# Bias off TensorE, transposes spread between matmuls, and a reordered first block in a gated SSM + MLP kernel

## Chip, cores, metric

One core of one Trainium2 chip. The metric is device microseconds of one execution. The span of a profiled run is some 1.7 us shorter than its time.

The profiles name the engines: PE is TensorE (PEld its weight loads), DVE VectorE, ACT ScalarE, POOL GpSimd, SP SyncE. PE writes into eight PSUM banks, `ps`; an eviction is the copy from a bank to SBUF. The granted clock is the share of full TensorE clock that the profile records. Names in the lines: `xnat` x as loaded, `xn` its layernorm, `xt` and `xnt` their transposes; `btres` B transposed; `u` the evicted B projection; `gt` the gelu output; `ht` the scanned state; `tq` the gated MLP output; `r` beside `in_A_C_re` or `in_A_C_im` a C load, one part of C; `wst` a staging buffer that holds a transposed part of C until it is stored to `ct_scratch`. A line that reads `[0.67 <-ACT xnt L428]` says that the engine was idle for 0.67 us before it, until that instruction. Some matmul records are missing from the traces, so x15 can stand for 16, with a gap of about 0.2 us in place of the missing one. The parts and items 1 to 7 are those of the prediction.

## The reference

```python
# x: 1 x 2048 x 1024 bf16; B_w1: 1024 x 3584; B_w2: 3584 x 1024
g = sigmoid((x * gate_w).sum(-1, keepdims=True))
# A: a diagonal complex recurrence between two complex projections
Bu   = einsum("bld,pd->blp", x, B_bar)
h[t] = Lam_bar * h[t-1] + Bu[:, t]                  # 2048 steps, 1024 channels
a    = 2 * einsum("blp,dp->bld", hseq, C).real + x * Dskip
# B: layernorm and an MLP
b    = gelu(layernorm(x) @ B_w1 + B_b1) @ B_w2 + B_b2
out  = g * a + (1 - g) * b
```

## The kernel before

The sequence is cut into four blocks of 512 rows. Each block runs `bu` (the B projection, 8 x 16 matmuls), `m1` (28 tiles, gelu on ScalarE), then for each half of the output columns `m2` (the second MLP matmul) and `my` (the C projection). VectorE runs the scan (`chain`). The first block also builds tables (Sin on ScalarE, products `CG` on VectorE) and transposes B (`bprep`) and C (`cprep`). Everything is ordered by hand: in the traces an instruction that waits also holds up those emitted after it on its engine (m_wst1 and i1_cload below show it for ACT and for the Pool queue).

```python
def load_x(self, b):                       # one transfer of 1 MB
    self.dma(q, ..., self.Xnat[:, :, :], src, writes=["xnat"])

def tx(self, b, part, banks=(6, 7)):       # 4 x 8 transposes, evicted by ACT
    for s in range(4):
        bank = banks[s % 2]
        ...

def cprep(self, i, banks):                 # one staging buffer
    ...
    Wst = self.Wst
    def t0(): ...ACT: Wst[:, 0, :] <- ps...
    def t1(): ...ACT: Wst[:, 1, :] <- ps..., then Pool queue: CTd <- Wst
    self.pending_act.extend([t0, t1])      # one is taken after each m1 tile

def m2(self, b, dblk, hook=None):
    def body0(h):                          # bias: ones (1 x 128) times b2row (1 x 512)
        for s in range(4):
            ins = h.matmul(self.ps[:, s, :], self.onesb[0:1, 0:128], self.b2row[...], start=True, stop=False)
    self.op(pe, body0, ..., writes=[f"ps{s}" for s in range(4)])
    for c in range(14):                    # 8 matmuls each
        ...
        if hook is not None and c == hook[0]: hook[1]()
    for s in range(4):                     # eviction by ACT
        self.op(act, lambda h: h.activation(self.TQ[s], self.ps[:, s, :], ACTF.Identity, scale=omg), ...)

# build(), cuts
cprep_at = {2: 0, 5: 1, 9: 2, 12: 3, 16: 4, 19: 5, 23: 6, 26: 7}   # m1 tile: C transpose
for b in range(NB):
    for i in range(8):
        ev = self.bu(b, i, defer_evac=(i >= 6))
        ...
    if b == 0: self.tx(0, 1, banks=(4, 5))
    for f in range(NF):
        self.m1(b, f)
        if deferred and f in (0, 4):
            i, ev = deferred.pop(0); ev()
            if b == 0 and i == 7: self.table_act(7); self.table_cg(7)
            self.chain(b, i)
        if b == 0 and f in cprep_at: ...   # after every second one: the next C load, Pool queue
    ...
    self.m2(b, 0); self.my(b, 0)
    self.m2(b, 1, hook=(6, all four transposes of xn))
    self.my(b, 1, hook=(0, all four transposes of x))
```

The table scratch lies in tiles 16 to 27 of the gelu output `gt`; the scratch of the products is gt tile 19, so the gelu of tile 19 must wait for the last `table_cg`.

Of the kernel before, what the change touches and what calls it, by code (L numbers as in the profile page):

```python
# [7 lines left out]
F32 = mybir.dt.float32  # L8
BF16 = mybir.dt.bfloat16
# [56 lines left out]
class _Builder:  # L66
# [96 lines left out]
    def alloc(self):  # L163
# [5 lines left out]
        self.rows = sb("rows", [64, 128], BF16)  # L169
        self.b2row = sb("b2row", [1, 1024], BF16)  # L170
        self.gwbc = sb("gwbc", [128, 1024], BF16)
# [44 lines left out]
        self.CTd = nc.dram_tensor("ct_scratch", [16, 128, 1024], BF16)  # L216

        self.psTb = [self.ps[:, k, :].bitcast(BF16) for k in range(8)]
        self.psT = [self.psTb[6], self.psTb[7]]
# [50 lines left out]
    def setup_rows_dma(self):  # L270
        rows = self.rows
        vecs = [(self.Lre_in, 0, 8), (self.Lim_in, 8, 8), (self.ldt_in, 16, 8), (self.Dsk_in, 24, 8), (self.b1_in, 32, self.NF)]
        items = [(rows[r0:r0 + n, :], ap.rearrange("(i p) -> i p", p=128), ["rows"]) for ap, r0, n in vecs]
        self.dma_group(self.sp, "d_rows", items)
        items = [(self.gwbc[:, :], self.gw_in.rearrange("(o n) -> o n", o=1).partition_broadcast(128), ["gwbc"]),
                 (self.b2row[:, :], self.b2_in.rearrange("(o n) -> o n", o=1), ["b2row"])]
        self.dma_group(self.act, "d_cst", items)
        self.mark_const("gwbc", "b2row")

# [94 lines left out]
    def load_x(self, b):  # L374
        src = self.x2[b * 512:(b + 1) * 512, :].rearrange("(s p) d -> p s d", p=128)
        q = self.sp if b == 0 else self.pool
        self.dma(q, "d_x" if b == 0 else "d_xp", self.Xnat[:, :, :], src, writes=["xnat"])

    def ln_stats(self, b):
        dve, pool = self.dve, self.pool  # L380
        Xn, XN = self.Xnat, self.XN
        for s in range(4):
            for hh in range(2):
                self.op(dve, lambda h, s=s, hh=hh: h.bn_stats(self.lnst[:, s, hh * 6:(hh + 1) * 6], Xn[:, s, hh * 512:(hh + 1) * 512]),  # L384
                        reads=["xnat"], writes=[f"lnst{s}"])
            self.op(dve, lambda h, s=s: h.bn_aggr(self.lnmv[:, s, :], self.lnst[:, s, :]), reads=[f"lnst{s}"], writes=[f"lnmv{s}"])
# [4 lines left out]
        for s in range(4):  # L391
            self.op(dve, lambda h, s=s: h.tensor_scalar(XN[:, s, :], Xn[:, s, :], self.lnmv[:, s, 0:1], self.rstd[:, s:s + 1],
                                                      ALU.subtract, ALU.mult),
                    reads=["xnat", f"lnmv{s}", "rstd"], writes=[f"xn{s}"])

    def gate_z(self, b):
        dve = self.dve
        Xn = self.Xnat
        for s in range(4):
            self.op(dve, lambda h, s=s: h.scalar_tensor_tensor(self.junk, Xn[:, s, :], 1.0, self.gwbc[:, :], ALU.mult, ALU.mult,  # L400
                                                             accum_out=self.zc[:, b % 2, s:s + 1]),
                    reads=["xnat", "gwbc"], writes=["q1", f"zc{b % 2}_{s}"])

# [8 lines left out]

    def tx(self, b, part, banks=(6, 7)):
        pe, act = self.pe, self.act
        src = self.Xnat if part == 0 else self.XN
        srcnames = ["xnat"] if part == 0 else [f"xn{s}" for s in range(4)]
        dst = self.XT if part == 0 else self.XNT
        dstname = "xt" if part == 0 else "xnt"
        for s in range(4):
            bank = banks[s % 2]  # L420

            def body(h, s=s, bank=bank):
                ins = None
                for k in range(8):
                    ins = h.transpose(self.psTb[bank][:, k * 128:(k + 1) * 128], src[:, s, k * 128:(k + 1) * 128], self.ident[:, :])  # L425
                return ins
            self.op(pe, body, reads=srcnames + ["ident"], writes=[f"ps{bank}"])
            self.op(act, lambda h, s=s, bank=bank: h.activation(dst[:, :, s * 128:(s + 1) * 128],  # L428
                                                               self.psTb[bank].rearrange("p (k n) -> p k n", k=8), ACTF.Identity),
                    reads=[f"ps{bank}"], writes=[dstname])  # L430

# [25 lines left out]
    def cprep(self, i, banks):  # L457
# [10 lines left out]
        nre, nim = f"ps{banks[0]}", f"ps{banks[1]}"  # L468
        Wst = self.Wst

        def t0():
            self.op(act, lambda h: h.activation(Wst[:, 0, :], pre, ACTF.Identity, scale=2.0), reads=[nre], writes=["wst_re"])

        def t1():
            self.op(act, lambda h: h.activation(Wst[:, 1, :], pim, ACTF.Identity, scale=-2.0), reads=[nim], writes=["wst_im"])
            dst = self.CTd.ap().rearrange("(c i) p d -> i p c d", c=2)[i]
            self.dma(pool, "d_ctw", dst, Wst[:, :, :], reads=["wst_re", "wst_im"], writes=[f"ctd{i}", f"ctd{8 + i}"])
        self.pending_act.extend([t0, t1])
# [121 lines left out]

    def m2(self, b, dblk, hook=None):
        pe, act = self.pe, self.act
        NC2 = self.NF // 2

        def body0(h):
            ins = None
            for s in range(4):
                ins = h.matmul(self.ps[:, s, :], self.onesb[0:1, 0:128], self.b2row[0:1, dblk * 512:(dblk + 1) * 512], start=True, stop=False)  # L608
            return ins
        self.op(pe, body0, reads=["onesb", "b2row"], writes=[f"ps{s}" for s in range(4)])  # L610
        for c in range(NC2):
            view, names = self.w2_load(dblk, c)
            last = (c == NC2 - 1)

            def body(h, c=c, view=view, last=last):
                ins = None
                for s in range(4):
                    for ff in range(2):
                        ins = h.matmul(self.ps[:, s, :], self.GT[:, 2 * c + ff, s * 128:(s + 1) * 128], view[:, ff, :],  # L619
                                       start=False, stop=(last and ff == 1))  # L620
                return ins
            self.op(pe, body, reads=names + [f"gt{2 * c}", f"gt{2 * c + 1}"], writes=[f"ps{s}" for s in range(4)])
            if hook is not None and c == hook[0]:
                hook[1]()
        for s in range(4):
            omg = self.omgcol[:, 4 * b + s:4 * b + s + 1]
            self.op(act, lambda h, s=s, omg=omg: h.activation(self.TQ[s], self.ps[:, s, :], ACTF.Identity, scale=omg),  # L627
                    reads=[f"ps{s}", f"omg{b}"], writes=[f"tq{s}"])

    def my(self, b, dblk, hook=None):  # L630
        pe, dve, act = self.pe, self.dve, self.act
        xt = self.XT

        def body0(h):
# [8 lines left out]
        for c in range(8):  # L643
# [10 lines left out]
            self.op(pe, body, reads=names + [f"ht{2 * c}", f"ht{2 * c + 1}"], writes=[f"ps{4 + s}" for s in range(4)])  # L654
            if hook is not None and c == hook[0]:
                hook[1]()
        for s in range(4):
# [7 lines left out]
    def build(self):  # L665
# [14 lines left out]
        self.bprep_load(6)  # L680
        self.bprep_load(7)
        self.setup_b()
        for i in range(8):
            self.table_dve(i)
        for c in range(3):
            self.w1_chunks[(0, c)] = self.w1_load(c)
        cprep_at = {2: 0, 5: 1, 9: 2, 12: 3, 16: 4, 19: 5, 23: 6, 26: 7}
        for b in range(NB):
            deferred = []
            for i in range(8):  # L690
# [3 lines left out]
                if b == 0:  # L694
                    if i + 2 < 8:
                        self.bprep(i + 2)
                    if i >= 1:
                        self.table_act(i - 1)
                        self.table_cg(i - 1)
                        if i - 1 <= 5:  # L700
                            self.chain(0, i - 1)
                    if i == 3:
                        self.setup_diag()
# [4 lines left out]
            if b == 0:  # L708
                self.tx(0, 1, banks=(4, 5))
            for f in range(NF):  # L710
                self.m1(b, f)
                if deferred and f in (0, 4):
                    i, ev = deferred.pop(0)
                    ev()
                    if b == 0 and i == 7:
                        self.table_act(7)
                        self.table_cg(7)
                    self.chain(b, i)
                if b == 0 and f in cprep_at:
                    ci = cprep_at[f]  # L720
                    self.cprep(ci, (6, 7) if ci % 2 == 0 else (0, 1))
                    if ci % 2 == 1 and ci + 1 < 8:
                        self.cprep_load((ci + 1) // 2)
            self.drain_act(len(self.pending_act))
# [10 lines left out]
            self.my(b, 0)  # L735
            hook_m2 = (6, (lambda b=b: self.tx(b + 1, 1, banks=(4, 5)))) if b + 1 < NB else None
            self.m2(b, 1, hook=hook_m2)

            def hook_fn(b=b):
                self.tx(b + 1, 0, banks=(0, 1))  # L740
            hook_my = (0, hook_fn) if b + 1 < NB else None
            self.my(b, 1, hook=hook_my)
            if b + 2 < NB:
                self.load_x(b + 2)
        fin = [_Tok(self.dma_sems[n], self.dma_counts[n], "dma") for n in self.dma_sems]
# [67 lines left out]
```

## Time and profile before

| | before |
|---|---|
| time, 6 runs | 706.22 us median (705.39 to 709.84) |
| span of the profiled run | 706.9 us |
| PE / DVE / ACT busy | 94% / 50% / 29% |
| first B projection, first m1, first m2 start (PE timeline) | 18.88, 58.68, 127.48 us |

The three starts divide the first block, where most of PE's listed waits lie (23.7 of 30.9 us). The prediction below shows the lines.

### The profile page before, as it was taken

Reading aid. Unit: us, or ns where it says so; the run is one execution under the profiler, and the core shown is the slowest. Engines: PE = TensorE matmul, PEld = TensorE weight load, DVE = VectorE, ACT = ScalarE, POOL = GpSimd, SP = SyncE. Lnnn points to the kernel's source line nnn. Section 1 sums busy time; section 2 is a strip of 40 time slices with the busy share of each in tenths; the row PEclk is TensorE's granted clock in tenths of the full one; section 3 lists DMA queues with packets and bytes.
Section 4 is the critical chain, followed back from the end, with each engine's and each line's share of the span. In section 5 each row is a group of like instructions: output and inputs, shape, how many; then the busy total and the mean of one; then the engine's idle time right before and its main releaser. Section 6 shows DMA issues by size and latency. Waiting matters only on the chain.

```text
span 706.9 us, 8889 instructions
## 1 busy us (share of the span) xinstructions
PE 667.2 (94%) x3489; PEld 317.0 (45%) x3489; DVE 351.0 (50%) x840; ACT 207.9 (29%) x281; POOL 38.2 (5%) x63
## 2 busy tenths in 40 slices
PE   3998898899999999999999999999999999999994
PEld 2554444344444444444444444444444444444442
DVE  4799998331005999811004999830102999300101
ACT  4886745110231243201231243301131233401010
POOL 1010121001001000000001000000101000000101
PEclk9999999899999999999999999999999999999998
DMA  8611676545435055444436045444534035444520
GB/s 282 210 61 45 226 252 228 203 149 167 131 97 172 1 147 151 149 150 154 142 96 203 0 117 151 150 151 148 164 105 149 0 89 151 149 153 146 175 64 30
DMA packets 113894, 97.33 MB, mean 138 GB/s; under 512 B 4923, under 2 KB 107323, under 8 KB 113852
## 3 DMA queue, kind: packets, MB, share of 16 engines
q1 hardware_dynamic: 109050, 80.77, 37.4%
q0 software_dynamic: 4656, 15.73, 6.0%
q8 instruction: 27, 0.44, 0.2%
q10 hardware_dynamic: 146, 0.26, 0.2%
q14 instruction: 15, 0.12, 0.1%
HBM read 88.36 MB, written 8.39 MB: 137 GB/s over the span
## 4 chain that ended last, share of the span: by engine, by line
PE 80%; DVE 13%; ACT 3%; DMA 2%; issue 1%; POOL 0%; DVEq 0%; ACTq 0%; POOLq 0%
PE ps L619 28%; PE ps L592 22%; PE ps L651 16%; PE ps L494 12%; DVE g L543 3%; PE ps L608 1%; DMA xnat<-in_A_x_dram 1%; PE ps L639 1%; PE ps L425 1%; ACT xt L428 1%; ACT xnt L428 1%; DVE lnst L384 1%; DVE p L518 1%; DVE q L549 1%; DVE p L519 1%
## 5 line engine op out<-in xcount | busy, mean ns | idle before, releaser
L592 PE MATMUL ps<-xnt,ring 128*128 128x512 bf16 x896 | 199.1, 384 | 7.1 <-ACT gt L597 5.4
L619 PE MATMUL ps<-ring,gt 128*128 128x512 bf16 x896 | 197.6, 382 | 0.0
L660 DVE SCALAR_TENSOR_TENSOR r<-ps,gcol,r 128x512 bf16<-128x512 f32 x32 | 21.8, 744 | 300.4 <-PE ps L651 300.4
L592 PEld LDWEIGHTS ps<-xnt,ring 128*128 128x128 bf16 x896 | 88.0, 99 | 113.8 <-issue 6.4
L619 PEld LDWEIGHTS ps<-ring,gt 128*128 128x128 bf16 x896 | 87.4, 98 | 108.7 <-issue 6.8
L597 ACT ACTIVATE gt<-ps,cst 128x512 bf16<-128x512 f32 x112 | 76.8, 687 | 128.4 <-PE ps L592 122.5
L494 PE MATMUL ps<-xt,btres 128*128 128x512 bf16 x512 | 113.5, 382 | 0.3 <-ACT btres L449 0.3
L651 PE MATMUL ps<-ring,ht 128*128 128x512 bf16 x512 | 112.3, 379 | 0.0
L494 PEld LDWEIGHTS ps<-xt,btres 128*128 128x128 bf16 x512 | 50.1, 99 | 60.2 <-issue 1.6
L651 PEld LDWEIGHTS ps<-ring,ht 128*128 128x128 bf16 x512 | 49.7, 98 | 57.8
L627 ACT ACTIVATE r<-ps,omgcol 128x512 f32<-128x512 f32 x32 | 19.4, 688 | 131.8 <-PE ps L619 131.8
L501 ACT ACTIVATE u<-ps 128x1024 bf16<-128x1024 f32 x32 | 32.7, 1023 | 83.3 <-PE ps L494 81.6
L543 DVE TENSOR_TENSOR_SCAN g<-dc,zmid,wb 128x256 bf16<-128x256 f32 x64 | 44.6, 738 | 1.1
L428 ACT ACTIVATE xnt<-ps 128x1024 bf16<-128x1024 bf16 x16 | 16.4, 1024 | 79.7 <-PE ps L425 78.6
L147 POOL DMA_DIRECT2D out_dram<-r x32 | 17.5, 547 | 392.5 <-DVE r L660 390.0
L543 DVE TENSOR_TENSOR_SCAN g<-dc,z,wb 128x256 bf16<-128x256 f32 x48 | 33.3, 734 | 0.0
L384 DVE BATCH_NORM_STATS2 lnst<-xnat 128x6 f32<-128x512 bf16 x32 | 21.5, 673 | 16.1 <-DMA xnat<-in_A_x_dram 15.5
L518 DVE TENSOR_TENSOR p<-u,CGre 128x1024 bf16<-128x1024 bf16 x32 | 22.0, 687 | 5.7 <-ACT u L501 5.3
L548 DVE TENSOR_TENSOR q<-g,Ere 128x1024 bf16<-128x1024 bf16 x32 | 22.1, 691 | 1.1
L425 PE MATMUL ps<-ident,xnat 128*128 128x128 bf16 x128 | 10.8, 242 | 12.2 <-DMA xnat<-in_A_x_dram 8.4
L519 DVE TENSOR_TENSOR p<-u,CGim 128x1024 bf16<-128x1024 bf16 x32 | 21.9, 684 | 0.0
L549 DVE TENSOR_TENSOR q<-g,Eim 128x1024 bf16<-128x1024 bf16 x32 | 21.9, 683 | 0.0
(104 smaller groups left out, 345.5 us busy)
## 6 DMA issues: line engine op xcount, KB each, us to landing
ring<-in_B_w_dram SPq DMA_DIRECT2D x56, 512.0 KB, 3.7
ring<-in_B_w_dram SPq DMA_DIRECT2D x112, 256.0 KB, 2.8
ring<-ct_scratch SPq DMA_DIRECT2D x64, 256.0 KB, 2.6
ct_scratch<-wst POOLq DMA_DIRECT2D x8, 512.0 KB, 4.0
out_dram<-r POOLq DMA_DIRECT2D x32, 128.0 KB, 2.3
xnat<-in_A_x_dram POOLq DMA_DIRECT2D x3, 1024.0 KB, 5.8
r<-in_A_C_re_dram POOLq DMA_DIRECT2D x4, 512.0 KB, 5.5
r<-in_A_C_im_dram POOLq DMA_DIRECT2D x4, 512.0 KB, 7.0
```

The costliest lines, as they stand in the source:

```text
L384: self.op(dve, lambda h, s=s, hh=hh: h.bn_stats(self.lnst[:, s, hh * 6:(hh + 1) * 6], Xn[:, s, hh * 512:(hh + 1) * 512]), reads=["xnat"], ...
L428: self.op(act, lambda h, s=s, bank=bank: h.activation(dst[:, :, s * 128:(s + 1) * 128], self.psTb[bank].rearrange("p (k n) -> p k n", k=8) ...
L494: ins = h.matmul(self.ps[:, 2 * pair + c, :], self.BTres[:, i, k, c * 128:(c + 1) * 128], xt[:, k, :], start=(k == 0), stop=(k == 7))
L501: self.op(act, lambda h: h.activation(self.U[u][:, :, :], self.ps[:, 2 * pair:2 * pair + 2, :], ACTF.Identity), reads=[f"ps{2 * pair}", f" ...
L518: self.op(dve, lambda h: h.tensor_tensor(v4(P1), v4(U), CGre_b, ALU.mult), reads=[f"u{u}", f"CG{i}"], writes=["p1"])
L519: self.op(dve, lambda h: h.tensor_tensor(v4(P2), v4(U), CGim_b, ALU.mult), reads=[f"u{u}", f"CG{i}"], writes=["p2"])
L543: self.op(dve, lambda h, c=c, init=init, hf=hf: h.tensor_tensor_scan(G[:, c, hf * TT:(hf + 1) * TT], rb, Wb[:, c, hf * TT:(hf + 1) * TT], ...
L549: self.op(dve, lambda h: h.tensor_tensor(v4(Q2), v4(G), Eim_b, ALU.mult), reads=[f"g{gs}_0", f"g{gs}_1", f"Ei{i}"], writes=["q2"])
L592: ins = h.matmul(self.ps[:, bank, :], view[:, k, ff * 128:(ff + 1) * 128], self.XNT[:, k, :], start=(k == 0), stop=(k == 7))
L597: self.op(act, lambda h: h.activation(self.GT[:, f, :], self.ps[:, bank, :], ACTF.Gelu_apprx_tanh, bias=b1c), reads=[f"ps{bank}", "cst"], ...
L619: ins = h.matmul(self.ps[:, s, :], self.GT[:, 2 * c + ff, s * 128:(s + 1) * 128], view[:, ff, :], start=False, stop=(last and ff == 1))
L651: ins = h.matmul(self.ps[:, 4 + s, :], self.HT[:, 2 * c + pp, s * 128:(s + 1) * 128], view[:, pp, :], start=False, stop=(last and pp == 1))
```

## The change

Intent: take the bias matmuls off PE (bias and gate factor are applied by DVE at the eviction), hide the evictions of the x transposes behind matmuls, start the first block sooner, and remove four stalls in the first `m1`.

```diff
-        self.b2row = sb("b2row", [1, 1024], BF16)
+        self.b2bc = sb("b2bc", [128, 1024], BF16)
+        self.ob = sb("ob", [128, 512], F32)
+        self.Wst2 = [self.R2[:, 0:1024]..., self.Wst]          # two staging buffers
 load_x:
-        self.dma(q, ..., self.Xnat[:, :, :], src, writes=["xnat"])
+        if b == 0:
+            for s in range(4):
+                self.dma(self.sp, f"d_x0{s}", self.Xnat[:, s, :], src[:, s, :], writes=[f"xnat{s}"])
 m2:
-        self.op(pe, body0, ...)                                 # bias matmuls
         for s in range(4):
-            self.op(act, ... activation(self.TQ[s], self.ps[:, s, :], Identity, scale=omg))
+            self.op(dve, ... tensor_scalar(self.ob, self.b2bc[...], omg, None, ALU.mult))
+            self.op(dve, ... scalar_tensor_tensor(self.TQ[s], self.ps[:, s, :], omg, self.ob, ALU.mult, ALU.add))
 build:
-        self.dma_group(self.act, "d_cst", [gwbc, b2row])        # first thing, ACT queue
+        self.dma_group(self.sp, "d_cst", [gwbc, b2bc])          # after the B loads, SP queue
-        cprep_at = {2: 0, 5: 1, 9: 2, 12: 3, 16: 4, 19: 5, 23: 6, 26: 7}
+        cprep_at = {0: (0, (6, 7)), 2: (1, (0, 1)), 8: (2, (6, 7)), 10: (3, (0, 1)),
+                    16: (4, (6, 7)), 18: (5, (0, 1)), 24: (6, (2, 3)), 26: (7, (6, 7))}
+        cload_after = {2: 1, 10: 2, 18: 3}
     table_act(7), table_cg(7): from m1 tile 4 to the end of the bu loop
-            if b == 0: self.tx(0, 1, banks=(4, 5))
+            if b == 0: self.tx(0, 1, banks=(4, 5, 6, 7))
-            self.m2(b, 1, hook=(6, tx)); self.my(b, 1, hook=(0, tx))
+            self.m2(b, 1, hooks={4: tx_s(0), 6: tx_s(1), 8: tx_s(2), 10: tx_s(3)})
+            self.my(b, 1, hooks={0: tx_s(0), 1: tx_s(1), 3: tx_s(2), 4: tx_s(3) and load_x})
```

## The prediction

> **What bounds the kernel now.** I read the busy shares first, then the waits of PE, the chain that ended last, the PE timeline, and busy time with granted clock in chosen stretches.
>
> ```profile
> PE 667.2 (94%) x3489; PEld 317.0 (45%) x3489; DVE 351.0 (50%) x840; ACT 207.9 (29%) x281; POOL 38.2 (5%) x63
> ```
>
> PE is busy for 667 of 706.9 us, so a gain has two sources only: PE work taken away, and PE idle or slow time taken away. The waits of PE list part of the second:
>
> ```profile
> PE ps L425 <- DMA xnat<-in_A_x_dram: 8.4, 1, 8.4
> PE ps L592 <- ACT gt L597: 5.4, 2, 2.7
> PE ps L425 <- ACT xnt L428: 4.7, 8, 0.7
> PE ps L425 <- ACT xt L428: 3.8, 7, 0.7
> PE ps L608 <- ACT thc L406: 2.9, 1, 2.9
> ...
> PE ps L464 <- DMA r<-in_A_C_im_dram: 1.0, 1, 1.0
> ```
>
> The chain in order of time says which of them carry the end. From 25 to 108 us it is DVE (tables and scan of the first block); at 108 us it passes to PE and stays there to 698 us:
>
> ```profile
> 107.53 0.49 DVE CGim L371
> ...
> 108.11 0.69 ACT gt L597
> ...
> 108.85 7.04 PE ps L592 x24
> ...
> 122.17 3.15 DMA ct_scratch<-wst
> ...
> 125.40 1.02 ACT wst L472
> 126.42 0.91 ACT wst L475
> 127.34 0.10 ACT thc L406
> ...
> 127.48 1.86 PE ps L608 x4
> ```
>
> Two handovers show. The gelu of tile 19 waits for the last table product (CGim of i=7), because that table's scratch lies in gt tile 19; and the last C transpose waits for a 3.15 us store out of the only staging buffer wst. The wait told as "thc" is really for the wst evictions that end just ahead of it: the bias matmul writes the banks they read, and never reads thc.
>
> After the first block PE runs without a gap except at the x transposes. One set in the PE timeline:
>
> ```profile
> 183.63 1.06 PE L425 MATMUL ps<-ident,xn 128*128 128x128 bf16 x16
> 185.36 0.62 PE L425 MATMUL ps<-ident,xn 128*128 128x128 bf16 x8 [0.67 <-ACT xnt L428]
> 186.47 0.62 PE L425 MATMUL ps<-ident,xn 128*128 128x128 bf16 x8 [0.49 <-ACT xnt L428]
> 186.93 12.25 PE L619 MATMUL ps<-ring,gt 128*128 128x512 bf16 x56
> ```
>
> It takes 3.30 us from first transpose to the next matmul, for 32 transposes on two banks, paced by 1.03 us evictions.
>
> **What the Trainium skill says.** "TensorE: Matmul & The Clock Gate", Part 1 (What's actually happening): the array runs at half clock after an idle window of about 3.4 us and needs about as long of activity to come back. The trace agrees that idle costs twice; columns are stretch, length, busy time of PE, PEld, DVE, ACT, POOL, granted clock, DMA share, GB/s:
>
> ```profile
> 108.85:115.70 6.85, 6.85 (x24) 2.78 (x25) 6.61 (x16) 3.84 (x5) 0.71 (x1) 0.75 0.79 261
> ...
> 127.48:129.34 1.86, 1.86 (x5) 0.47 (x6) 0.22 (x2) 0.00 (x0) 1.49 (x2) 0.50 0.26 106
> ```
>
> 24 matmuls took 7.04 us after the stall at 108.85 against 5.34 us elsewhere: 1.7 us lost. Here gaps of 2.6 and 2.9 us sufficed. Same page, Part 2 (Back-to-back issue gap): 216 ns for N=512. The trace has 24.28 us for 112, 217 ns. "ScalarE: Activation LUTs", What ACT_TABLE_LOAD costs: 1283 ns a load. The trace agrees with 1.28 us, at 72.63 and again at 75.11, around the Sin of i=7 in the midst of the gelus. "DMA: Bandwidth & Descriptors", Anatomy of one DMA: about 2 us fixed plus size over bandwidth, so a quarter of x should land well ahead of the whole. Here 256 KB land in 2.8 us, and the first x (1 MB) in 7.5.
>
> **The change part by part.**
>
> 1. Bias matmuls of m2 go. They stand in the chain as seven of 0.96 us and one of 1.86 us (half clock): 8 x 0.96 = 7.7; the 0.9 of slow clock is counted in 4. Saved: 7.7 us.
>
> 2. Transposes spread. Sixteen take 0.89 us (the C transposes, 115.73 to 116.62), so eight take 0.45. Four lots cost 1.8 us against 3.30, if no lot waits for its bank. A bank comes round again after four chunks in m2 and three in my (8 matmuls, 1.73 us each), so after 5.2 us or more, against an eviction of 1.03. 1.5 us x 6 sets = 9.0 us.
>
> 3. First block, m1. The list of stalls between 58.68 and 127.48: 2.75 at 77.14 (ACT behind two table loads), 0.99 at 97.36 (C load), 2.62 at 108.85 (table product on DVE), 2.90 at 127.48 (wst). Sin of i=7 moves ahead of the first gelu, which takes two of three loads out of the way; its product now comes before chain 6, so 8.2 us earlier on DVE (106.17 to 98.0). C loads get six m1 tiles (10.4 us) instead of three or four (issue to landing 7.0 at worst by the median row, and some 8 with its Pool issue). wst has two buffers, and the last C transposes leave banks 0 and 1 alone. As a whole: m1 after the change is 28 x 1.727 = 48.4, eight C transposes 7.1, cold start as before 1.7, sum 57.2 us; before it was 68.8. Saved: 11.6 us, of which 9.3 are the stalls and 1.7 the cold clock at 108.85.
>
> 4. First m2. Without the 2.9 us gap the clock should stay up: 26.6 back to 24.28, and the 0.9 of the bias: 3.2 us.
>
> 5. Start. x in quarters with gwbc (256 KB) out of its way. In the stretch 4 to 5 us the DMA moved only 115 GB/s while gwbc ran beside x, against 400 later. I estimate the first quarter at 4.3 us instead of 8.31. Then DVE's path (statistics 1.53 us a quarter, rstd, xn, cst at 17.78, so 9.5 us after x) starts 4.0 us sooner if each next quarter lands within 1.5 us. PE's first projection waits for cst through the bank of the small transpose, so it moves from 18.88 to about 14.9. Saved: 4.0 us.
>
> 6. Four banks for the first xnt set: ACT is the limit there (four evictions 4.37 us of the 5.16), and three more activations stand ahead. Nothing.
>
> 7. Added: on DVE 32 multiplications ob (0.35 us, from the 128x256 rows and the 540 ns of a 1024 wide one) and 32 evictions of 0.74 (the row of L660). 1.1 x 4 = 4.4 us at each m2's end, when DVE is idle (302.9 to 333.1 in block 1). The result is needed 14.9 us later. Nothing.
>
> Sum: 7.7 + 9.0 + 11.6 + 3.2 + 4.0 = 35.5, so 706.2 - 35.5 = 670.7. Check from below: m1 starts at 54.7, m2 at 111.9, plus 24.2 x 2 + 14.7 x 2 + 3.6 = 81.4 gives 193.3; blocks 1 and 2 at 27.6 + 48.4 + 81.4 = 157.4 give 508.1; the last 153.8, then the tail from 698.0 to 706.9 of 8.9: 670.8. I say 671.
>
> **The rivals.** (a) Block 0 stays on DVE. DVE is over 90% busy from 25 to 116 us, and a quicker PE may just wait for it at another place. Against: the only late ties from DVE to PE are the scratch in gt 19 (free at 99.9 in the old frame, PE needs it at about 102) and ht, needed 24 us after chain 7. If it held, up to 5 us of item 3 stay: 676. (b) The startup is bound by the sum of early loads and the queue's issue (0.45 us each, three more in front of B), not by x. B and rows are due only 3 us later, but if x's quarters land like the whole, item 5 is 1 us: 674. (c) DMA in the first m1 becomes the bound: busy share 0.69 to 0.81 there, and the same bytes in 57 instead of 69 us make about 0.85. The ring holds 20 us of weights, which speaks against. It would cost 2 to 5 us: 675. (d) Clock: PE's idle before the first m1 becomes one piece of some 3.3 us instead of three, so the cold start may double: 1.7 us, 672. (e) Spread transposes wait or break the weight preload: if all of item 2 is lost, 680. Against: the diagonal matmuls, also 128 wide, sit between big ones at 0.89 per 16 without a gap.
>
> **Range and chances.** 7.7 + 9.0 are near certain and alone give 2.4%. Items 3 to 5 are certain in direction and open by some 6 us together, mostly upwards. 671, range 667 to 678. All rivals at once give about 688, still faster by over 2%: 0.97; within 2% 0.02, slower 0.01 for something unseen.
>
> **What would show it right or wrong.** Item 1: no L608 group. 2: each set adds 0.45 x 4, no PE wait on xnt or xt after the first block. 3: PE waits on gt, C_im and wst gone; first m1 57 us long. 4: first m2 24.3 us at clock 1.0. 5: first transposes at 4.3, first projection at 14.9. 7: DVE done with tq 5 us after each m2, no wait of PE for it. Wrong it would be if PE shows new waits in the first m1 (on DVE or ring loads), if the clock is low at the first m2, or if x's first quarter lands after 6 us.

## The result, and the profile after

673.32 us median (672.0 to 675.24, 8 runs) against 706.91 (705.39 to 709.9, 16 runs). The ratio is 0.9521, 95% interval 0.9501 to 0.954: 33.9 us of 706.9. The spans of the two profiles differ by 706.9 - 671.4 = 35.5 us. That this is the forecast sum to the tenth is luck: the run profiled before the change took 708.64 us, 1.7 us above the median.

| | before | after | gained up to here |
|---|---|---|---|
| first B projection starts | 18.88 | 13.93 | 4.95 |
| first m1 starts | 58.68 | 54.09 | 4.59 |
| first m2 starts | 127.48 | 112.66 | 14.82 |
| first my starts | 155.77 | 136.84 | 18.93 |
| end | 706.9 | 671.4 | 35.5 |

PE fills the span almost wholly; DVE has more to do, ACT less. From the page of the changed kernel:

```profile
PE 648.0 (97%) x3457; PEld 313.1 (47%) x3457; DVE 389.9 (58%) x904; ACT 185.7 (28%) x247; POOL 38.3 (6%) x63
```

Its waits of PE (total, times, longest):

```profile
PE ps L428 <- DMA xnat<-in_A_x_dram: 4.9, 2, 3.4
PE ps L599 <- ACT xnt L431: 3.2, 1, 3.2
PE ps L471 <- DMA r<-in_A_C_im_dram: 2.6, 3, 1.2
PE ps L501 <- ACT btres L456: 1.8, 1, 1.8
...
```

The listed waits of before sum to 31 us, these to 14.5, and none of them is on gt, on the staging buffer, or on a transpose after the first block. Three are larger than before: the xnt wait ahead of the first m1 (1.7 to 3.2), the C load (1.0 to 2.6) and btres (0.3 to 1.8). The PE timeline shows them (start, length, line, count, idle time ahead):

```profile
45.47 3.63 PE L501 MATMUL ps<-xt,btres 128*128 128x512 bf16 x16 [1.85 <-ACT btres L456]
48.93 1.95 PE L428 MATMUL ps<-ident,xn 128*128 128x128 bf16 x32
54.09 1.89 PE L599 MATMUL ps<-xnt,ring 128*128 128x512 bf16 x8 [3.21 <-ACT xnt L431]
...
105.69 1.07 PE L471 MATMUL ps<-ident,r 128*128 128x128 bf16 x16 [1.17 <-DMA r<-in_A_C_im_dram]
...
112.66 24.34 PE L620 MATMUL ps<-ring,gt 128*128 128x512 bf16 x112
```

The last line answers to the 26.65 us of the first m2 before: no slow clock. The next three answer to the set of transposes before, part of a set spread through m2; no bracket, so no wait:

```profile
164.08 0.61 PE L428 MATMUL ps<-ident,xn 128*128 128x128 bf16 x8
164.52 3.62 PE L620 MATMUL ps<-ring,gt 128*128 128x512 bf16 x16
167.98 0.61 PE L428 MATMUL ps<-ident,xn 128*128 128x128 bf16 x8
```

A lot costs 164.52 - 164.08 = 0.44 us. On DVE the last eviction of the first m2 ends at 145.01 + 0.75 = 145.8 us, and PE needs its banks at 151.54, so the added 39 us of DVE work (351.0 to 389.9) stay off the path. This set ends 8.9 us after its m2 (136.84), not 5, because DVE was still at the next block's gate; there were 14.7 us.

### The profile page after: what moved, and what is told of

Read it like the earlier page. A ratio compares the mean times of both kernels' runs of the same rounds, so it can differ in the third digit from the quotient of the medians. Undisturbed runs are those within 1.5% of the kernel's fastest.

```text
span 671.4 us, 8856 instructions
## 1 busy us (share of the span) xinstructions
PE 648.0 (97%) x3457; PEld 313.1 (47%) x3457; DVE 389.9 (58%) x904; ACT 185.7 (28%) x247; POOL 38.3 (6%) x63
## 4 chain that ended last, share of the span: by engine, by line
PE 88%; issue 5%; DMA 3%; POOL 1%; DVE 1%; ACT 0%; DVEq 0%; SPq 0%; POOLq 0%
PE ps L620 29%; PE ps L599 23%; PE ps L655 16%; PE ps L501 15%; DMA r<-in_A_C_im_dram 3%; PE ps L428 2%; PE ps L643 1%; PE ps L451 1%; DMA xnat<-in_A_x_dram 1%; PE ps L471 1%; POOL r L158 1%; DVE lnst L389 0%; POOL ct_scratch L147 0%; DVE xn L397 0%; POOL out_dram L147 0%
## 5 line engine op out<-in xcount | busy, mean ns | idle before, releaser
L599 PE MATMUL ps<-xnt,ring 128*128 128x512 bf16 x896 | 195.3, 379 | 3.2 <-ACT xnt L431 3.2
L655 PE MATMUL ps<-ring,ht 128*128 128x512 bf16 x512 | 113.8, 379 | 0.0
L630 DVE SCALAR_TENSOR_TENSOR r<-ps,omgcol,ob 128x512 f32<-128x512 f32 x32 | 24.0, 751 | 152.9 <-PE ps L620 151.9
L431 ACT ACTIVATE xt<-ps 128x1024 bf16<-128x1024 bf16 x16 | 16.4, 1024 | 41.1 <-PE ps L428 40.9
```

Of the source, the lines that this page charges most:

```text
L431: self.op(act, lambda h: h.activation(dst[:, :, s * 128:(s + 1) * 128], self.psTb[bank].rearrange("p (k n) -> p k n", k=8), ACTF.Identity) ...
L599: ins = h.matmul(self.ps[:, bank, :], view[:, k, ff * 128:(ff + 1) * 128], self.XNT[:, k, :], start=(k == 0), stop=(k == 7))
L630: self.op(dve, lambda h, s=s, omg=omg: h.scalar_tensor_tensor(self.TQ[s], self.ps[:, s, :], omg, self.ob[:, :], ALU.mult, ALU.add), reads= ...
L655: ins = h.matmul(self.ps[:, 4 + s, :], self.HT[:, 2 * c + pp, s * 128:(s + 1) * 128], view[:, pp, :], start=False, stop=(last and pp == 1))
```

## The experiments

Four kernels undo one part each (two of them with a part that hangs on it), four divide two of these parts further, three try to remove what the changed kernel still waits for. Part 6 was not undone. A difference of ratios is turned into us with 706.9. The 95% intervals of the ratios are 0.002 to 0.004 to either side (1.3 to 3.0 us), so differences of 1 or 2 us rest on the traces, one of each kernel, and not on the times.

### u1_bias: parts 1 and 7 undone

```diff
+        self.op(pe, body0, reads=["onesb", "b2row"], ...)       # bias matmuls again
-            self.op(dve, ... ob ...); self.op(dve, ... TQ ...)
+            self.op(act, ... activation(self.TQ[s], self.ps[:, s, :], Identity, scale=omg))
```

> The changed kernel with part 1 and part 7 undone: bias matmuls on PE again, m2 evicted by ACT, everything else as changed. Theory (PE carries the end after the first block, and the DVE evictions cost nothing): 8 x 0.96 us come back, so span 671.4 + 7.7 = 679.1 us, all of it as eight PE groups of 0.96 us, none at half clock, since no idle comes before the first. Rival (the DVE evictions and the shared scratch ob delay something, so taking them away gives a part back): less than 6 us longer. Rival (the first one is slow as it was before the change): 8.6 us or more.

Measured: 681.91 us (681.35 to 682.47), ratio 0.9651, so 9.2 us more than the changed kernel; span 679.6, 8.2 more. From its PE groups by shape (count, busy us, mean ns, idle ahead):

```profile
L615 PE MATMUL ps<-b2row,onesb 1*128 1x512 bf16 x32 | 8.3, 377 | 0.0
```

The first group of four takes 0.96 us like the others. So the bias costs about what PE needs for it (7.7 reckoned, and both differences lie within the noise of that), and moving the eviction to DVE neither costs nor gives anything that shows. A matmul with a contraction of one row takes as long here (377 ns) as one of 128 rows (379).

### u2_lump: part 2 undone

```diff
-                self.m2(b, 1, hooks={4: ..., 6: ..., 8: ..., 10: ...})
-                self.my(b, 1, hooks={0: ..., 1: ..., 3: ..., 4: ...})
+                self.m2(b, 1, hooks={6: lambda: self.tx(nb, 1, banks=(4, 5))})
+                self.my(b, 1, hooks={0: lambda: self.tx(nb, 0, banks=(0, 1))})
```

> The changed kernel with part 2 undone: the four transposes of a set stand together again on two banks. Theory: each of the six sets takes 3.30 us instead of 1.8, so 9.0 us longer, span 680.4, with PE waits on xnt and xt of 0.67 and 0.50 us again in every set. Rival (part of the gain of spreading came from loading x earlier or from a shorter wait elsewhere): clearly other than 9.0, with PE waits in other places.

Measured: 682.93 us (681.6 to 683.7), ratio 0.966, 9.8 us more; span 679.9, 8.5 more. The waits are back in every set, with the lengths of before:

```profile
163.04 1.06 PE L428 MATMUL ps<-ident,xn 128*128 128x128 bf16 x16
164.76 0.62 PE L428 MATMUL ps<-ident,xn 128*128 128x128 bf16 x8 [0.67 <-ACT xnt L431]
165.88 0.62 PE L428 MATMUL ps<-ident,xn 128*128 128x128 bf16 x8 [0.49 <-ACT xnt L431]
```

This run also holds a lesson on the first block: its first projection ran slow (5.27 us against 3.62 in the trace of the changed kernel, though the clock recorded for that stretch is 1.00, so that record doesn't show every slow stretch), yet there is no wait before the last projection here, where the changed kernel has 1.85 us, and m1 starts at 54.64 against 54.09. PE's time there doesn't set the start of m1; something else does. i2_nu5 takes that up.

### u3_start: part 5 undone

```diff
-            for s in range(4): self.dma(self.sp, f"d_x0{s}", ...)
+            self.dma(self.sp, "d_x", self.Xnat[:, :, :], src, ...)
-        self.cst_items = items
+        self.dma_group(self.act, "d_gw", items[:1])             # gate weights first again
+        self.cst_items = items[1:]
```

> The changed kernel with the start undone: x as one transfer, gate weights broadcast first on the ACT queue (the bias broadcast stays late). Theory: the first projection goes from 13.93 back to about 18.9 us, and since the trace after the change shows PE waiting 1.85 us for DVE through the buffers u before the last projection in both cases, the first m1 starts 4.6 us later: span about 676 us. Rival (DVE sets the pace of the first block, and its chain starts 4.5 us earlier too, so the loss is exactly DVE's shift): the same number but with the wait before the last projection unchanged. Rival (the slow clock in the first projection comes back with the late start): 1.2 us more in it, 0 to 1.2 us more in the span.

Measured: 678.09 us (677.01 to 678.28), ratio 0.9591, 4.9 us more; span 676.4, 5.0 more. First projection at 18.97, first m1 at 58.88 against 54.09: 4.8 us. There is no wait before the last projection, as in u2_lump with a slow first projection (5.08 us here), so it isn't the same "in both cases" as I had written. The start is worth 4.8 us at m1.

### s1_quarters and s2_late: the two halves of part 5

s1 keeps the quarters and puts the gate weights first; s2 keeps the gate weights late and loads x whole.

> The changed kernel, x still in quarters, but the gate weights broadcast early on the ACT queue, beside x. With s2 it divides the 4.9 us of the start. Theory (both halves count: a quarter releases work early, and the broadcast slows x): first transposes at about 4.4 instead of 3.4, statistics held up by late quarters, first projection at about 15.5 against 13.9, first m1 about 1.5 us later, span about 673. Rival (the quarters do it all): as the changed kernel within 0.5 us, first projection at 14. Rival (the broadcast does it all): first projection above 17.5, span about 675.5.

> The changed kernel with x as one transfer, but the gate weights late as in the change. Theory (both count): x whole lands at about 6.3 instead of 8.0, first projection at about 17.2, first m1 3 us later than in the changed kernel, span about 674.5. Rival (quarters do it all): as with the whole start undone, first projection at 18.9, span 676.4. Rival (the broadcast does it all): first projection at 14, span 671.5.

| | gate weights late | gate weights first |
|---|---|---|
| x in quarters | changed: statistics from 3.38, projection at 13.93, m1 at 54.09 | s1: 5.92, 16.89, 56.79 |
| x whole | s2: 6.28, 17.25, 57.45 | u3: 8.00, 18.97, 58.88 |

s1: 676.1 us, ratio 0.955; s2: 676.18 us, ratio 0.955. Both rivals, that one of the two does it all, fall by the starts of m1: each half is worth 1.4 to 3.4 us, depending on the other, and both together 4.8. The times alone would not decide it, since the intervals of these ratios overlap that of the changed kernel. The size in s1 was off: I expected the first quarter at 4.4, and it comes at 5.92 (the first statistics on DVE, from the timelines of s1 and of the changed kernel):

```profile
5.92 1.42 DVE L390 BATCH_NORM_STATS2 lnst<-xnat 128x6 f32<-128x512 bf16 x2 [5.92 <-DMA xnat<-in_A_x_dram]
```

```profile
3.38 1.42 DVE L389 BATCH_NORM_STATS2 lnst<-xnat 128x6 f32<-128x512 bf16 x2 [3.38 <-DMA xnat<-in_A_x_dram]
```

A 256 KB broadcast beside it delays a 256 KB quarter by 2.5 us.

### u4_m1: part 3 undone, and with it part 4

```diff
-        cprep_at = {0: ..., 2: ..., 8: ..., 10: ..., 16: ..., 18: ..., 24: ..., 26: ...}
+        cprep_at = the tiles and banks of before; C loads after tiles 5, 12, 19
-        Wst, (wre, wim) = self.Wst2[i % 2], self.Wst2_names[i % 2]
+        Wst, (wre, wim) = self.Wst2[1], self.Wst2_names[1]
     table_act(7), table_cg(7) back at m1 tile 4
```

> The changed kernel with part 3 undone: last table in the midst of the gelus, one staging buffer, the old schedule of C transposes and C loads. Theory: the stalls of 2.75, about 1, 2.6 and 2.9 us come back, against 2.6 us of C load waits that go: 6.7 us of stalls, plus slow clock after them of 1.7 us in m1 and 2.3 in the first m2: 10 to 13 us, span 681 to 684. Rival (the stalls are there but the clock stays up, as the slow stretches were chance): 6 to 8 us, span 677 to 679.

Measured: 684.58 us (681.67 to 684.79), ratio 0.9676, 11.0 us more; span 682.8, 11.4 more. From its waits of PE:

```profile
PE ps L599 <- ACT gt L604: 5.3, 2, 2.7
...
PE ps L620 <- ACT thc L411: 2.9, 1, 2.9
...
PE ps L471 <- DMA r<-in_A_C_im_dram: 1.0, 1, 1.0
```

The four stalls are back at their old lengths (2.74, 2.58, 2.94, 1.03), and so are the slow stretches after two of them: 24 matmuls (23 records) in 7.04 us after 104.03 at a clock of 0.75, and a first m2 that is 25.6 us long (122.70 to 148.29) where 2.3 us of slow clock were expected and about 1.4 came. That favours the theory over "the slow stretches were chance", though one of its runs took only 681.67 us at a mean clock of 0.992 where the others had 0.983 to 0.987.

### m_t7 and m_wst1: two pieces of part 3 alone

m_t7 puts only the last table back at tile 4; m_wst1 only takes the second staging buffer away.

> The changed kernel with only the last table put back in the midst of the gelus (tile 4) and its product behind chain 6 on DVE; two staging buffers and the new schedule stay. Theory: two of the four stalls come back, about 2.7 us at tile 6 or 7 (two ACT table loads of 1.28 us, the three activations, behind evictions of the C transposes that are now there too, so perhaps 3.5), and at tile 21 a wait for the product, which ends about 103 on DVE while PE would be there at about 101: 1 to 3 us. C load waits shrink by what PE comes later. Span 674 to 678. Rival (the schedule of the C transposes made the stalls): none of the two, 671.5.

> The changed kernel with one staging buffer again; last table and schedule as changed. Theory (a single buffer costs only where the bank it holds is needed at once): with the pairs of C transposes 3.5 us apart, each second eviction waits for a store of 3.9 us, ACT is strictly in order, so the gelu behind it is late and PE stalls 1 to 3 us in each of four pairs but the last: 3 to 8 us, span 674 to 679, with PE waits on gt. Rival (evictions have the slack): under 1 us, span 671.5 to 672.5.

m_t7: 678.42 us (678.37 to 679.98), ratio 0.9591, 4.9 us more. PE waits on gt twice, 3.64 us at tile 7 and 2.74 at tile 21 (6.4 in sum), and the C load waits fall from 2.6 to 0.8. The ACT timeline shows the cause of the first:

```profile
67.85 1.28 ACT L359 ACT_TABLE_LOAD   x1
...
70.33 1.28 ACT L604 ACT_TABLE_LOAD   x1
71.63 1.26 ACT L604 ACTIVATE gt<-ps,cst 128x512 bf16<-128x512 f32 x2
```

m_wst1: 677.33 us (676.99 to 678.37), ratio 0.9572, 3.6 us more. PE waits on gt four times, 5.2 us in sum, and no longer on any C load. From its waits of ACT:

```profile
ACT wst L479 <- DMA ct_scratch<-wst: 10.3, 4, 2.8
```

So ACT stands still for the store, and the gelu behind it is late. The new schedule, with its close pairs of C transposes, needs the second buffer: the old one lost 2.9 us to a single buffer, at the end of m1 alone, this one 5.2.

### i1_cload: the C load ahead of the store on the Pool queue

```diff
-        cprep_at = {0: ..., 2: (1, (0, 1)), 8: ..., 10: (3, (0, 1)), 16: ..., 18: (5, (0, 1)), 24: ..., 26: (7, (6, 7))}
-        cload_after = {2: 1, 10: 2, 18: 3}
+        cprep_at = {0: ..., 1: (1, (0, 1)), 8: ..., 9: (3, (0, 1)), 16: ..., 17: (5, (0, 1)), 24: ..., 25: (7, (6, 7))}
+        cload_after = {1: 1, 9: 2, 17: 3}
```

> The changed kernel with the second C transpose of each pair one m1 tile earlier (tiles 0 and 1, 8 and 9, 16 and 17, 24 and 25) and the next C load right behind it. Theory (the C load waits because its issue stands on the Pool queue behind the store of the first transpose, which waits for ACT): the load is now queued ahead of that store, some 2.5 to 3.6 us sooner, and all C load waits of PE (2.6 us in the changed kernel's trace) vanish: span 669. Rival (the load is late because the DMA engines are full): it lands only about as late as before, waits of 1.5 us or more stay, span 671.

Measured: 671.63 us (671.33 to 671.81), ratio 0.9499, 1.6 us less than the changed kernel; span 670.1. The intervals of the two ratios overlap, but no run of one kernel lies among those of the other (671.81 at most, 672.0 at least). PE has no C load wait left. The Pool timeline of the changed kernel, then of i1_cload:

```profile
62.26 0.71 POOL L147 DMA_DIRECT2D ct_scratch<-r  x1 [19.42 <-ACT r L482]
62.97 0.92 POOL L158 DMA_DIRECT2D r<-in_A_C_re_dram  x1
63.88 0.88 POOL L158 DMA_DIRECT2D r<-in_A_C_im_dram  x1
```

```profile
61.55 0.88 POOL L158 DMA_DIRECT2D r<-in_A_C_re_dram  x1 [17.22 <-PE ps L471]
62.42 0.88 POOL L158 DMA_DIRECT2D r<-in_A_C_im_dram  x1
64.65 0.71 POOL L147 DMA_DIRECT2D ct_scratch<-r  x1 [1.34 <-ACT r L482]
```

In the changed kernel the store stands first and waits for ACT, and the load behind it waits too, though the buffer it needs was read for the last time at about 61.1 us, where the transposes end (the next matmuls start at 61.06). Put first, the load also lands faster: 4.9 and 5.7 us (median, re and im) against 7.0 and 8.4. So the im load gains 1.5 us by its earlier issue and 2.7 by its shorter way. The store that now stands behind it pays: 6.5 us (median) from issue to landing, against 3.9. The mean busy share of the DMA engines in the first m1, 0.72 against 0.74, hides how full they are while these loads are under way. From the issue of the load above to its landing (for i1_cload by the median), changed kernel and then i1_cload; the last three columns are granted clock, DMA share and GB/s:

```profile
62.97:72.26 9.29, 8.61 (x40) 3.72 (x39) 8.84 (x23) 6.71 (x9) 2.51 (x4) 1.00 0.96 275
```

```profile
61.55:68.12 6.57, 6.57 (x32) 2.96 (x31) 6.20 (x15) 5.31 (x8) 2.49 (x4) 1.00 0.87 254
```

So full engines aren't excluded as the reason for the longer way behind the store; what i1_cload shows is that the order is enough to remove the wait. The span falls by 1.3 us, not 2.6, because this trace had slow clock in its first m1 (its first 8 matmuls took 3.02 us against 1.89, the 16 transposes after them 1.63 against 1.06); no pair of traces without that difference came out of these runs.

### i2_nu5: one more u buffer

```diff
-        self.NU = 4
+        self.NU = 5
```

> The changed kernel with five u buffers instead of four. Theory (the wait of 1.85 us before the last projection of the first block is DVE's, handed on by ACT through the u buffers, so PE's lead at the start is partly given back): PE has no wait there, ACT none on p, first m1 starts up to 1.85 us sooner (52.2 in a trace whose first projection runs at full clock, about 53 to 53.5 in one where it starts slow), span 669.5 to 671. Rival (the evictions of bprep are late by themselves): the wait stays, 671.5.

Measured: 673.55 us (672.78 to 675.39), ratio 0.9532 (0.9506 to 0.9557): no gain. Yet the wait it was made for is gone: PE has none before the last projection, ACT none for a u buffer, and m1 starts at 52.99 instead of 54.09. That lead was lost within m1. Its waits of PE:

```profile
PE ps L599 <- ACT xnt L431: 3.2, 1, 3.2
PE ps L471 <- DMA r<-in_A_C_im_dram: 2.4, 2, 1.8
...
```

Slow clock at the start of m1 took some 1.7 us (8 matmuls in 3.21 us against 1.89, 16 transposes in 1.44 against 1.06). The C waits in sum did not grow (2.4 against 2.6), but the last one did, from 1.17 to 1.81 us: it ends at 106.04 against 105.69 and sets the start of the first m2, 113.02 against 112.66. So the mechanism of the theory holds (the lead of PE is held up by DVE through the u buffers). Its size in the end time is nothing in these runs, with the later C wait standing; what it would be at full clock, no run shows.

### i3_best: all three

NU = 5, the schedule of i1_cload, and two more edits:

```diff
+                if b == 0 and i >= 6:                  # two of the four lots ahead of each of the last two projections
+                    for s in (2 * i - 12, 2 * i - 11): self.tx_s(0, 1, s, 4 + s)
-            if b == 0: self.tx(0, 1, banks=(4, 5, 6, 7))
     scratch of the table products: gt tile 19 -> gt tile 27
```

> Both of the above, and xnt of the first block transposed between the last two projections instead of after them, with the last product's scratch moved from gt tile 19 to tile 27 so that an earlier PE does not meet it. Theory: the 3.2 us wait for xnt before the first m1 goes too, m1 starts at about 49 to 50 instead of 54.1, no waits in it: span 663 to 665, ratio to the kernel before about 0.941. Rival (DVE sets the first block's pace): new waits of PE on gt, ht or on DVE's evictions at the first m2, and a span over 667.

Measured: 667.36 us (667.35 to 667.77), ratio 0.9442 (0.942 to 0.9463), output correct: 5.6 us less than the changed kernel, 39.4 less than before. m1 starts at 50.96, m2 at 107.26. In its waits of PE nothing over 0.4 us is left after the first projection. The span is 666.0, one above the range I gave; its first projection took 5.60 us (clock 0.79 from 13.9 to 24 us) where the changed kernel's profiled run had 3.62. How the 5.6 us divide among the edits was not measured.

## Why the prediction was right

| part | predicted | undone, by span | undone, by ratio |
|---|---|---|---|
| 1 and 7, bias and eviction | 7.7 | 8.2 | 9.2 |
| 2, transposes | 9.0 | 8.5 | 9.8 |
| 3 and 4, first m1 and first m2 | 11.6 + 3.2 | 11.4 | 11.0 |
| 5, start | 4.0 | 5.0 | 4.9 |
| sum | 35.5 | 33.1 | 34.9 |

The sum of the four is the whole (33.9 by ratio, 35.5 by span) within the spread of single runs, some 1.5 us each. So the parts add, within that spread, and the mechanism of parts 1, 2 and 4 was right. Parts 3 and 5 each had a step wrong, and in the sum these errors partly cancelled: undone, parts 3 and 4 come to 11 and not 14.8, part 5 to 5 and not 4. Step by step:

- Item 1 was right; the eight groups are what comes back. The 216 ns cited beside it is, in that section of the skill, the gap of an isolated matmul; for a stream of weight loads and matmuls the section gives about 131 ns, which this trace, at 217 ns over 112 of them, doesn't bear out.
- Item 2 was right: 3.30 us to four lots of 0.44 to 0.45.
- Item 3 was right in the stalls that go and wrong in one term: I reckoned six tiles (10.4 us) enough for the C load. It comes to 2.6 us of waits, since the load is issued behind the store (i1_cload removes them all), and is 8.4 us under way and not 7.0 (median, im). What saved the sum is that the 1.7 us of cold start in m1, which I had kept, didn't occur in the profiled run: 58.6 us measured, 57.2 predicted. That was luck; i1_cload and i2_nu5 had it.
- Item 4 was right: m2 took 24.3 us, at full clock.
- Item 5 was too small for the first projection (4.95 us against 4.0; the first quarter came at 3.4, not 4.3), but 4.6 us reached m1. The first projection was also 1.2 us shorter than before (3.62 against 4.84), and this gain, with the rest, went into a wait that I hadn't seen: ACT stood 3.3 us for a u buffer that DVE had not read, and PE 1.85 us behind ACT.
- Item 6 was right: 3.21 us of waiting in one piece instead of three, m1 at the same distance from the last projection.
- Item 7: ob takes 485 ns, not 350, so a set of evictions is about 5 us, not 4.4. It cost nothing, as said.

Of the rivals, (a) held in a small form: DVE does set PE's pace in the first block, not at gt 19 as I had looked for, but through u, for 1.85 us. (b) falls with u3 and its halves. (c) came true in its sign, 2.6 us of C load waits, at a mean DMA share of 0.74 in the first m1 and not 0.85. That the same bytes can't be moved in a shorter m1 falls with i1_cload, which moves them in 57.4 us without a C load wait; whether the engines are too full for store and load at once stays open (0.96 busy over the first load, 0.87 in i1_cload). (d) is chance from run to run: after the same pause before m1 the changed kernel's trace is at full clock and that of i1_cload isn't. (e) falls. "All rivals at once" is summed wrong: 5 + 3 + 4 + 1 + 9 = 22, so 693 us and not 688, which is 1.9% faster and not over 2%.

## What to carry to other kernels

Where one engine is busy 94% of the time, list its waits and its own avoidable work, check that each lies on the chain that ends last, and add them up; here the sum held to 2 us, in part by luck. A removed wait is worth only what the next wait on the same path leaves of it: one more buffer gained 1.1 us at m1 and nothing at the end, where the C load behind it was still late. On an in-order queue, put the transfer that someone will wait for ahead of one that itself still waits.

## What the Trainium skill lacked or had wrong

- "TensorE: Matmul & The Clock Gate", Part 1 (What's actually happening), puts the return to half clock at an idle window of about 3.4 us or more. Here it followed pauses of 2.62 us (before) and 2.58 us (u4_m1), 24 matmuls taking 7.04 us each time, while after 2.75 us in the same run of before 24 took 5.35. After the pause of 3.2 us before m1, the first 8 matmuls took 1.89 us in one run and 3.02 in another. The page also says that the window runs freely, so where it falls may matter; no run here shows what decides it, and the figure is no safe bound.
- "DMA: Bandwidth & Descriptors", Anatomy of one DMA, gives a fixed and a per-byte part for a transfer issued from GpSimd, and has nothing on what a broadcast of one 2 KB row to 128 partitions does to its neighbours. Here 256 KB of it beside x moved the first statistics, which wait for the first quarter, from 3.38 to 5.92 us (s1_quarters), and with the whole x from 6.28 to 8.00 (s2_late, u3_start).
